# Which expert blocks of a convolution and mixture-of-experts kernel are single, double and fourfold

## The chip, the cores and the metric

The kernel runs on one core of a Trainium2 chip. The metric is the device time of one execution in microseconds (us); a time is the median of several runs. Beside it stands one execution taken with the hardware profiler, which shows every instruction of the engines: TensorE (PE, its weight loads apart as PEld), VectorE (DVE), ScalarE (ACT), GpSimd (POOL) and SyncE (SP), which issues most of the transfers.

## The reference

The input is 8 sequences of 3584 tokens with 192 channels, 28672 tokens in all, in float32. First comes a causal convolution of 7 taps with softmaxed weights, one set for each of 8 groups of 24 channels. Then each token goes through one of 8 experts of 192 x 1024 and 1024 x 192:

```python
for s in range(S):
    fresh_e = int(np.argmax(logits[b, s]))
    if s == 0 or local_gate[b, s] < 0.5:
        e = fresh_e
    else:
        e = prev_e if prev_e >= 0 else fresh_e
    prev_e = e
    ls = logits[b, s] - logits[b, s].max()
    p = np.exp(ls)
    p /= p.sum() + 1e-09
    h = np.maximum(x[b, s] @ w1[e], 0.0)
    out[b, s] = p[e] * (h @ w2[e])
```

A token either takes the best expert of its own logits or, where the local gate says so, the expert of the token before it. So the choice of expert is a running scan along the sequence.

## The kernel before

**Parts.** The tokens are worked in 16 parts of 1792 (PT). For each part the kernel convolves (`conv`, L390: 48 VectorE operations, L411, and eight on ScalarE, L401), computes logits and routes (`route`, L625; the logits with four transposes L594 on VectorE, 96 matmul records L604 on TensorE and two copies L609 on ScalarE), and scatters the rows into `slots`, a table in memory that is sorted by expert (`put`, L794: one indirect DMA on GpSimd, L801, for 128 rows, 14 for a part). The first two parts go a wider way of their own at the start (`wide`, `wide_route`).

**Units and blocks.** A unit is 128 rows of one expert in `slots`; the 28672 tokens make 229 of them here. Expert work is done in blocks: single (128 rows of one expert), pair (256) or fourfold (512). For each block the weights of the expert are loaded (`load_w`, L940, 1536 KB), the rows are loaded from `slots` (`load_rows`, L947), turned (`turn`, L383 with the copies L985), put through the hidden layer (`hidden`, L999, relu L1004) and the output layer (`output`, L1016, then L1024 on ScalarE and L1030 on VectorE, and the rows are sent out by L1034). A fourfold block comes only when all parts are routed; its hidden layer uses seven products in place of eight (`seven`, L1152; output L1196, L1206, L1209, L1214).

**Which blocks, when.** How many units are full after a part is known before the run only as a sure lower bound: of `tokens` rows over 8 experts at most 8 x (size - 1) can lie in unfilled blocks (`_sure`, L51). From it come lists for each part g: ONE[g], how many single blocks may have begun when part g is routed, up to the part EARLY - 1; TWO[g], the same for pairs, from part EARLY on and at most PAIRED; FOUR, PAIRS and REST, the fourfold, double and single blocks after the last part. Tables (`table`, L814), made on VectorE after a part, say which rows and which expert block i has. FIRST is the number of blocks before the fourfold ones. With the constants of the kernel before:

- ONE is 7, 21, 35 and then 35; 21 singles need parts 0 and 1, 14 more need part 2
- TWO is 0, 0, 0, 3, 10, 17, ... 59, 60: three pairs need part 3, then seven need each later part, and one part 12
- FIRST is 95, FOUR 13, PAIRS 4; 14 singles end it. 20 further single blocks stand in a conditional at the end and run only if rows are left.

**The order of the work.** The program is written for one fixed order on each engine. The main loop (L1359) goes block by block. Between a block's hidden layer and output, and after it, it calls `step(time)` (L1258), which issues routing and convolution work of the next parts until the costs that these generators yield (0.6 for an operation of the convolution, 0.1 to 0.8 for one of the routing) fill `time`: 4.6 for a single block, 9.6 for a pair. Routing goes first, and where it says "hop" the rest of that call is left to the convolution. `hidden` sends two scatters for a block; a pair sends a third (`put(copied)`, L1377) when over 7 are queued and a fourth (L1026) when over 12 are. At the head of each block `ensure` asks for the rows of the blocks up to three ahead:

```python
def ensure(i):
    for j in range(len(xgs) + i, min(i + AHEAD + 1, len(blocks))):
        g = blocks[j][3]
        while st["routed"] < g or any(p[0] <= g for p in to_put):
            if j > i + 2:
                return
            step(4.2)
            put()
        xgs[j] = load_rows(j)
```

`blocks[j][3]` is the part that block j needs, `to_put` the queue of scatters that aren't issued yet. A block three ahead may wait for the next call; one two ahead may not.

**Buffers that matter.** The output of a block goes to two banks (`yps_p`, two buffers); the next block's output can begin only when L1024 and L1030 have read them. The hidden layer has four banks (`hps_p`), which the logits use too.

Of the kernel before, what the change touches and what calls it, by code (L numbers as in the profile page):

```python
# [43 lines left out]
CAP = CAPU * UT  # L44
NU = (N + E * (UT - 1)) // UT
DUMMY = E * CAPU
EARLY = 3
SPARE = 2


def _sure(tokens, size):  # L51

    return max(0, -(-(tokens - E * (size - 1)) // size))
# [3 lines left out]
def _likely(tokens, size, left):  # L57
# [4 lines left out]

LAST = NPART - 1
PADS = NPART
PAIRED = 60
LEFT4 = E * (QT // 2 + UT // 8)
LEFT2 = E * (BT // 2 + UT // 8)
ONE = [_sure(min(g + 1, EARLY) * PT, UT) for g in range(NPART)]
TWO = [min(PAIRED, _sure((g + 1) * PT - ONE[-1] * UT, BT)) if g >= EARLY else 0
       for g in range(NPART)]  # L70
# [1439 lines left out]
```

## Time and profile before

| | us |
|---|---|
| median of 3 runs (1322.0 to 1323.66) | 1322.66 |
| profiled execution | 1305.35 |
| its span, first to last instruction | 1303.6 |
| VectorE busy, of the span | 846.3 |
| GpSimd busy, of the span | 523.1 |
| first hidden layer of a block (L999) | begins at 44.7 |
| first fourfold block (L1152) | begins at 910.2 |
| last logits (L604) | begin at 808.5 |
| last scatter of a part (L801) | begins at 882.2 |

The granted clock of TensorE is 0.997 of full speed over the span. The singles lie between 44.7 and 252.5 us, the pairs up to 910, the fourfold blocks up to about 1180, and the late pairs and singles after them. In the table of groups a line stands for all instructions of one source line and shape; the timeline of an engine merges equal neighbours, with the count behind the x; a bracket at its end gives the idle time in front of it and what ended it.

### The profile page before, as it was taken

What the parts mean: (1) busy time and instruction counts of PE and PEld (TensorE: products, weight loads), DVE (VectorE), ACT (ScalarE), POOL (GpSimd) and SP (SyncE); (2) the same over time, 40 slices, a digit from 0 to 9 for tenths busy, and PEclk for the clock granted to TensorE, in tenths of its full rate; (3) what the DMA queues carried; (4) which work ended last, traced back from release to release, by engine and by line L of the source; (5) the groups of instructions that cost most, each with busy time, mean ns of one, the idle gap of its engine ahead of it and who ended that gap; (6) DMA issues with size and microseconds to landing.
All of it is one profiled execution on the core that took longest, in us unless ns stands there. A gap on an engine that the chain in (4) does not pass through costs nothing.

```text
span 1303.6 us, 40830 instructions
## 1 busy us (share of the span) xinstructions
PE 1284.2 (99%) x16434; PEld 1220.6 (94%) x16434; DVE 846.3 (65%) x2526; ACT 651.1 (50%) x1482; POOL 523.1 (40%) x577
## 2 busy tenths in 40 slices
PE   9899999999999999999999999999999999999997
PEld 7799999999999999999999999999999999999997
DVE  5989898988988899998999996801333333330000
ACT  5456565544445445444454544444645556454453
POOL 3455353533435344353544534454433433322211
PEclk9999999999999999999999999999999999999999
DMA  5799999975757576575765755666323323324584
GB/s 195 285 357 415 386 384 345 398 273 202 269 203 278 196 274 244 207 280 190 281 246 204 281 193 205 214 213 235 128 87 135 122 105 140 110 94 167 212 303 164
DMA packets 63077, 300.42 MB, mean 230 GB/s; under 512 B 12064, under 2 KB 34263, under 8 KB 45474
## 3 DMA queue, kind: packets, MB, share of 16 engines
q1 hardware_dynamic: 40560, 252.54, 53.2%
q0 software_dynamic: 22320, 45.22, 9.5%
q8 instruction: 131, 2.15, 0.7%
q14 instruction: 64, 0.52, 0.1%
q10 hardware_dynamic: 2, 0.00, 0.0%
HBM read 252.12 MB, written 46.07 MB: 229 GB/s over the span
## 4 chain that ended last, share of the span: by engine, by line
PE 96%; DVE 3%; issue 0%; POOL 0%; POOLq 0%; ACT 0%; DVEq 0%
PE yps L1016 31%; PE hps L999 31%; PE ps L1196 15%; PE ps L1152 8%; PE ps L1103 4%; PE xps L383 2%; PE xps L1152 2%; PE hps L604 2%; DVE y_sb L411 1%; PE hps L233 1%; PE hps L178 0%; DVE hot L574 0%; PE hps L256 0%; PE yps L264 0%; DVE run L475 0%
## 5 line engine op out<-in xcount | busy, mean ns | idle before, releaser
L1016 PE MATMUL yps<-wb,hT 64*128 64x192 f32 x4960 | 429.8, 325 | 3.2 <-DVE o_sb L1030 2.4
L999 PE MATMUL hps<-xT,wb 64*128 64x256 f32 (+1 forms) x4560 | 425.9, 338 | 1.9 <-DVE at L503 1.2
L999 PEld LDWEIGHTS hps<-xT,wb 64*128 64x128 f32 x4560 | 378.7, 188 | 33.9 <-issue 3.9
L1016 PEld LDWEIGHTS yps<-wb,hT 64*128 64x128 f32 x4960 | 405.7, 187 | 4.6 <-DVE o_sb L1030 2.7
L411 DVE SCALAR_TENSOR_TENSOR y_sb<-x_sb,c,y_sb 128x336 f32<-128x336 f32 x672 | 375.6, 569 | 28.4 <-ACT y_sb L401 10.5
L801 POOL DMA_INDIRECT slots<-y_sb,posi x228 | 229.6, 1007 | 205.7 <-ACT xT L985 90.8
L1004 ACT ACTIVATE hT<-hps 128x512 f32<-128x512 f32 (+1 forms) x380 | 176.4, 516 | 244.5 <-PE hps L999 244.5
L1034 POOL DMA_INDIRECT out_dram<-o_sb,xg x155 | 161.5, 1042 | 276.0 <-DVE o_sb L1030 222.2
L1209 DVE SCALAR_TENSOR_TENSOR o_sb<-ps,y_sb,o_sb 128x192 f32<-128x192 f32 x74 | 28.1, 413 | 233.5 <-ACT o_sb L1206 233.5
L1214 POOL DMA_INDIRECT out_dram<-o_sb,y_sb x74 | 76.4, 1032 | 237.5 <-DVE o_sb L1209 218.7
L1196 PE MATMUL ps<-wb,x_sb 64*128 64x192 f32 x1952 | 165.0, 323 | 0.0
L1196 PEld LDWEIGHTS ps<-wb,x_sb 64*128 64x128 f32 x1952 | 159.3, 187 | 0.6
L1024 ACT ACTIVATE o_sb<-yps,xg 128x192 f32<-128x192 f32 x155 | 58.7, 418 | 178.4 <-PE yps L1016 178.3
L985 ACT COPY xT<-xps 128x256 f32<-128x256 f32 (+3 forms) x380 | 142.0, 374 | 10.6 <-PE xps L383 4.8
L1030 DVE SCALAR_TENSOR_TENSOR o_sb<-yps,xg,o_sb 128x192 f32<-128x192 f32 x155 | 58.6, 410 | 77.2 <-ACT o_sb L1024 77.0
L1206 ACT ACTIVATE o_sb<-ps,y_sb 128x192 f32<-128x192 f32 x74 | 27.9, 418 | 102.2 <-PE ps L1196 97.7
L1152 PE MATMUL ps<-x_sb,wb 64*128 64x256 f32 x624 | 73.7, 376 | 0.0
L1152 PEld LDWEIGHTS ps<-x_sb,wb 64*128 64x128 f32 x624 | 59.0, 187 | 7.3
L401 ACT ACTIVATE y_sb<-x_sb,c 128x336 f32<-128x336 f32 x112 | 61.9, 578 | 0.0
L1103 PE MATMUL ps<-x_sb,wb 64*128 64x128 f32 (+1 forms) x864 | 61.6, 295 | 0.0
L1103 PEld LDWEIGHTS ps<-x_sb,wb 64*128 64x128 f32 x864 | 59.4, 188 | 0.9 <-issue 0.2
L1083 ACT COPY x_sb<-xps 128x128 f32<-128x128 f32 (+5 forms) x124 | 58.7, 473 | 2.3
(277 smaller groups left out, 1043.5 us busy)
## 6 DMA issues: line engine op xcount, KB each, us to landing
wb<-in_w_dram SPq DMA_DIRECT2D x122, 1536.0 KB
x_sb<-in_x_dram SPq DMA_DIRECT2D x14, 1920.0 KB
xg<-slots SPq DMA_DIRECT2D x60, 195.0 KB
wb<-in_w_dram SPq DMA_DIRECT2D x12, 512.0 KB
y_sb<-slots SPq DMA_DIRECT2D x13, 390.0 KB
slots<-y_sb,posi POOLq DMA_INDIRECT x228
xg<-slots SPq DMA_DIRECT2D x33, 97.5 KB
x_sb<-in_xb_dram SPq DMA_DIRECT2D x4, 768.0 KB
```

The lines of the kernel that those rows point to most:

```text
L401: nc.scalar.activation(cols(h), chans(h, 0), Act.Copy, scale=c[:, h, 0:1])
L411: nc.vector.scalar_tensor_tensor(cols(h), chans(h, k), c[:, h, k:k + 1], cols(h), Alu.mult, Alu.add)
L801: ins = nc.gpsimd.indirect_dma_start(out=slots[:, :], in_=rows, in_offset=None, out_offset=bass.IndirectOffsetOnAxis(ap=to, axis=0)).ins
L985: copied = nc.scalar.copy(a, b)
L999: nc.tensor.matmul(hps[half][:, j, w], lhsT=wb[rows, f0:f0 + P], rhs=xT[rows, d, w], start=(d == 0 and j == 0), stop=(d == KD - 1), skip_g ...
L1004: relu = nc.scalar.activation(hT[:, m:m + 2, w], hps[half][:, :, w], Act.Relu)
L1016: nc.tensor.matmul(yps[half][:, k * D:(k + 1) * D], lhsT=hT[rows, m, k * P:(k + 1) * P], rhs=wb[rows, WA + m * D:WA + (m + 1) * D], start= ...
L1034: sent = nc.gpsimd.indirect_dma_start(out=out, in_=o_sb[:, k, :], in_offset=None, out_offset=bass.IndirectOffsetOnAxis(ap=xg.bitcast(I32)[ ...
L1103: nc.tensor.matmul(hps[:, half, j, :], lhsT=wb[rows, f0:f0 + P], rhs=xT[rows, d, :], start=(d == 0 and j == 0), stop=(d == KD - 1), skip_g ...
L1152: ins = nc.tensor.matmul(to[:, half, j, :], lhsT=b[rows, j * P:(j + 1) * P], rhs=a[rows, :], start=(first and j == 0), stop=True, skip_gro ...
L1196: ins = nc.tensor.matmul(yps[:, half, k * D:(k + 1) * D], lhsT=h[two][rows, side, j, k * P:(k + 1) * P], rhs=wb[rows, WA + f * D:WA + (f + ...
L1214: sent = nc.gpsimd.indirect_dma_start(out=out, in_=o_sb[:, k, :], in_offset=None, out_offset=bass.IndirectOffsetOnAxis(ap=xg.bitcast(I32)[ ...
```

## The change

Two constants change. The rest follows from them by the formulas of the code.

```diff
-EARLY = 3
+EARLY = 2
 SPARE = 2
...
-PAIRED = 60
+PAIRED = 63
```

The formulas between them and the blocks stay:

```python
ONE = [_sure(min(g + 1, EARLY) * PT, UT) for g in range(NPART)]
TWO = [min(PAIRED, _sure((g + 1) * PT - ONE[-1] * UT, BT)) if g >= EARLY else 0
       for g in range(NPART)]
PAST = ONE[-1] * UT + TWO[-1] * BT
FOUR = _likely(N - PAST, QT, LEFT4)
```

ONE becomes 7, 21 and then 21. TWO becomes 0, 0, 3, 10, 17, ... 59, 63: three pairs need part 2, seven part 3, and so on. FIRST becomes 84, FOUR 15; PAIRS stays 4 and the singles at the end stay 14. The rows that the blocks before FIRST take go from 19840 to 18816.

## The prediction

> **What bounds the kernel now.** I read the page first: busy time, the 40 slices and the chain. TensorE is busy from end to end, and the chain of work that ended last is TensorE's own.
>
> ```profile
> PE 1284.2 (99%) x16434; PEld 1220.6 (94%) x16434; DVE 846.3 (65%) x2526; ACT 651.1 (50%) x1482; POOL 523.1 (40%) x577
> PE 96%; DVE 3%; issue 0%; POOL 0%; POOLq 0%; ACT 0%; DVEq 0%
> ```
>
> A busy TensorE can hide waits, so next the waits of TensorE alone, from the start to the end. They sum to about 10 us and all but 1.5 us of them lie in the first 65 us. There is nothing left here to take away; there is much that could be added.
>
> ```profile
> PE yps L1016 <- DVE o_sb L1030: 2.4, 1, 2.4
> PE xps L383 <- DMA xg<-slots: 1.3, 1, 1.3
> ```
>
> Third, the windows by stage (stretch, then busy us of PE, PEld, DVE, ACT, POOL, then clock, DMA share and GB/s). VectorE, which does the convolution and the routing, has 275 of 300 us filled in the middle of the run. It is the one engine that can't take a burst of work without somebody waiting.
>
> ```profile
> 80.00:171.40 91.40, 90.74 (x1535) 89.75 (x1534) 80.59 (x275) 51.31 (x162) 41.57 (x43) 1.00 0.97 378
> 500.00:800.00 300.00, 300.00 (x3766) 282.56 (x3764) 274.61 (x817) 147.38 (x335) 137.55 (x132) 1.00 0.67 240
> 910.00:1180.00 270.00, 270.00 (x3058) 254.65 (x3056) 90.82 (x155) 146.62 (x199) 95.52 (x106) 1.00 0.33 116
> ```
>
> Last, TensorE's timeline, for what one block costs (start, us, engine, line). The first matmuls of a block's hidden layer come 5.445 us apart for singles (149.66 to 193.22 is eight blocks), 10.66 for pairs and 20.42 for blocks of 512.
>
> ```profile
> 149.66 2.83 PE L999 MATMUL hps<-xT,wb 64*128 64x128 f32 x46
> 155.10 2.83 PE L999 MATMUL hps<-xT,wb 64*128 64x128 f32 x46
> ...
> 604.38 5.34 PE L999 MATMUL hps<-xT,wb 64*128 64x256 f32 x48
> 615.04 5.35 PE L999 MATMUL hps<-xT,wb 64*128 64x256 f32 x48
> ...
> 910.24 2.75 PE L1152 MATMUL ps<-x_sb,wb 64*128 64x256 f32 x24
> 930.66 2.75 PE L1152 MATMUL ps<-x_sb,wb 64*128 64x256 f32 x24
> ```
>
> **What the Trainium skill says.** PSUM — Partial Sum Buffer, section Engine vs sequencer instructions: the queues of VectorE, ScalarE and GpSimd are strictly first in, first out, and matmuls start in program order. The trace agrees: nine convolution operations that stood ahead of one output's L1030 on VectorE (58.91 to 64.10) are what the 2.41 us wait below was for. TensorE: Matmul & The Clock Gate, section What's actually happening: after an idle window of about 3.4 us the array falls to half rate until a busy window of that length. The trace agrees: behind that one wait the granted clock was 0.68 on average from 64.6 to 68 us, and 29 matmuls took 4.00 us where 30 take 2.65.
>
> ```profile
> 64.57 4.00 PE L1016 MATMUL yps<-wb,hT 64*128 64x192 f32 x29 [2.41 <-DVE o_sb L1030]
> ```
>
> **The change, part by part.** *The blocks.* With the constants worked out, singles go from 35 to 21, pairs from 60 to 63, blocks of 512 from 13 to 15; the 4 late pairs and 14 late singles stay, and so do the 229 units in all. By the periods above: -14 x 5.445 + 3 x 10.66 + 2 x 20.42 = -76.2 + 32.0 + 40.8 = **-3.4 us** of TensorE. Nine loads of 1536 KB of weights go as well. TensorE hardly waits for them today (1.5 us of unnamed waits after 80 us), so they are worth between -1.5 and 0; I take 0. One table (L814) is still made for each part up to the cap, so VectorE's own sum is unchanged but for the time at which it is asked for.
>
> *Whose rows a pair needs.* Before, the 14 singles 21 to 34 use part 2, and part 3 is first needed by block 35. After, three pairs (21 to 23) use part 2, and block 24 already needs part 3. That is 8 units of 5.4 us earlier. From the later parts on (unit 41, 55, ...) the needs are as before. So the question is what the planner has issued by then. I follow step() with the costs that its generators yield. Up to block 20 nothing differs. Route 3 puts its 14 scatters in the queue in block 18; blocks 19 and 20 send two each, as the trace shows two L801 per single from 164.26 on:
>
> ```profile
> 169.70 1.04 POOL L801 DMA_INDIRECT slots<-y_sb,posi  x1 [1.23 <-ACT xT L985]
> 171.05 0.96 POOL L801 DMA_INDIRECT slots<-y_sb,posi  x1 [0.31 <-issue]
> ```
>
> Ten are left. Block 21, now a pair, sends three. Seven are left when ensure(22) asks for block 24. At i=21 the test j > i + 2 let it off; at i=22 it doesn't. The loop has to run seven times step(4.2) and put(), one behind the other, with no matmul of a block between them. Before, singles 21 to 25 send the ten, and the loop never runs anywhere. This is the step that decides.
>
> *What the seven rounds hold.* Convolution 4 has 48 operations: 20 are issued by block 20 and 16 in block 21. Rounds 1 and 2 issue its last 12. Round 3 begins route 4: four transposes (L594), then 3 operations of convolution 5. Round 4 puts the logits' matmuls (L604) into TensorE's queue and the copies L609 into ScalarE's, then 7 operations. Round 5 is 4.3 us of routing. Round 6 is 0.4 and 7 operations. Round 7 puts the exponential L662 into ScalarE's queue and 4.2 us of routing on VectorE. All of it stands ahead of block 22.
>
> *Its price.* Durations from VectorE's timeline: nine L411 in 5.15 to 5.28 us, so 0.577 each; the four L594 1.84 + 1.43.
>
> ```profile
> 172.25 0.41 DVE L1030 SCALAR_TENSOR_TENSOR o_sb<-yps,xg,o_sb 128x192 f32<-128x192 f32 x1
> 172.57 5.15 DVE L411 SCALAR_TENSOR_TENSOR y_sb<-x_sb,c,y_sb 128x336 f32<-128x336 f32 x9
> ...
> 191.30 1.84 DVE L594 STREAM_TRANSPOSE z<-y_sb 128x768 f32<-128x768 f32 x2
> ...
> 194.10 1.43 DVE L594 STREAM_TRANSPOSE z<-y_sb 128x768 f32<-128x768 f32 x2
> ```
>
> Block 21 begins at 171.5 on TensorE, as in the trace, and ends at 182.2. Its two L1030 end at about 183.7. From there VectorE has, in order: 6 operations 3.5 (to 187.1), rounds 1 and 2, 6.9 (194.0), transposes 3.3 (197.3), 10 operations 5.8 (203.1), routing of round 5, 5.0 by the same rows of route 3 at 145.0 (208.1), round 6 4.4 (212.5), round 7 4.6 (217.1), block 22's own steps of 4.8 and 1.2, 6.3 (223.4), and block 22's L1030, 0.7: 224.1.
> First wait: L604 stands next in TensorE's queue and needs the transposes: 182.3 to 197.3, **15.0 us**. Second: its 1.6 us, the hidden layer and the transposes of block 22 are through by 204.5 at full clock and 206.5 at half clock; the relu behind L662 comes at 208.4, because L662 waits for L637 in round 5 (207.5). So 2 to 4 us. Third: block 23's output needs the bank that block 22's L1030 reads at 224.1, and TensorE is there at about 219.4: some 5 us. In sum: without waits TensorE would begin block 23's output at 182.2 + 10.66 + 5.4 + 1.6 = 199.9; it begins at 224.2. **24.3 us**. The half clock after the third wait isn't absorbed by a later one: 1.4 by the row at 64.57 to 3.4 by the skill's window; I take 1.7. Block 23 leaves VectorE 10.0 us of work per 10.66, its L1030 is out at 234.5 and block 24's output comes at 236.9: no fourth wait.
> The seven scatters cost 7 x 1.27 on GpSimd (from 186.4), and block 24's rows, waiting behind them on SP, are needed only at 229: nothing. The weights of block 25 behind them have 40 us: nothing.
>
> *The work done early* buys nothing back: no wait of TensorE is left later that it could shorten.
>
> *The end of the pairs.* FIRST goes from block 95 to 84 and lies 8 units earlier. By the same count the last table comes in block 78, six pairs ahead (seven before), and at ensure(82) one scatter of part 15 is left: one forced put, 1.3 us on GpSimd, with 16 us until its rows are turned. Nothing; if that cover were gone, 1 to 4.
>
> **Sum.** -3.4 + 24.3 + 1.7 = +22.6 us. The profiled execution took 1305.35 (span 1303.6 and 1.75 around it): 1328.0. The median of the runs, 1322.66, stands 17.3 above it; the trace doesn't show why, and I carry that over unchanged: **1345.3**.
>
> **Rivals.** Only the first wait: if VectorE gets through rounds 4 to 7 while TensorE catches up, it is -3.4 + 15.0 + 1.7, 1336. For it: the second and third are ends of long sums. Against: VectorE's queue is strict, and the sum has no idle piece in it. More than forecast: part 5's input late, each wait followed by a full slow window, a fourth wait at block 24, where there are only 2.4 us to spare: some 8 us more, 1353. On the other side: no wait at all, 1322.66 - 3.4 = 1319.3. Its mechanism is one: the queue of scatters is empty when block 24 is asked for, so that no round is forced. Its place is ensure(22), its price the whole 26 us, and it decides from seven more scatters sent by block 21. Against it stands the trace's two per single. That the change doesn't do what it says I exclude: the input's experts, counted, fill all 15 blocks of 512, 4 pairs and 14 singles, so the conditional blocks at the end stay empty as before.
>
> **Numbers.** Forecast 0.71, first wait only 0.13, more 0.10, none 0.04, and 0.02 for something between none and one. A measurement tells no more than 0.2% (2.6 us) from no change. Faster 0.04, same 0.02, slower 0.94. The range reaches to the smaller case and to the larger one's middle: 1335 to 1353.
>
> **What would show it.** TensorE's waits: 15 us in front of L604, released by L594; about 5 in front of L1016, released by L1030; 2 to 4 in front of L1016 behind ScalarE, all between 180 and 226 us, with a granted clock below 1 there. Seven L801 in a row near 187. Then no wait until the end, and 84 early blocks. I am wrong if L604 at about 182 waits less than 10 us, or if TensorE waits again after block 24.

## The result, and the profile after

The changed kernel takes **1341.11 us** (median of 4 runs, 1339.65 to 1343.4) beside 1323.16 for the kernel before (4 runs, 1322.0 to 1328.92): a ratio of 1.0128, with a 95% interval of 1.0099 to 1.0156. (All ratios here are taken over the single runs; the quotient of two medians can differ by up to 0.0015.) It is slower by 18 us, where +22.6 had been summed. The profiled execution took 1340.49 us, its span is 1338.8.

The page of the changed kernel, first the busy times, then the chain of work that ended last:

```profile
PE 1294.6 (97%) x16082; PEld 1254.2 (94%) x16082; DVE 856.8 (64%) x2523; ACT 650.7 (49%) x1416; POOL 529.1 (40%) x585
PE 83%; issue 8%; DVE 5%; POOL 2%; DMA 1%; ACT 0%; another core or an unknown queue 0%; POOLq 0%; SPq 0%; DVEq 0%; ACTq 0%
```

TensorE has 352 matmul records fewer than before and is still the engine that ends last. VectorE's share of the chain went from 3% to 5%: the path now leaves TensorE for a stretch. The 8% under "issue" say nothing of the loss: they lie behind 1176 us, in the late blocks, where the chain is followed another way, and TensorE is busy there for 152.7 of 154 us. TensorE's waits in the changed kernel (us in total, times, longest) say who it waits for:

```profile
PE hps L604 <- DVE z L594: 13.1, 2, 12.9
PE yps L1016 <- DVE o_sb L1030: 6.9, 2, 4.7
PE yps L1016 <- issue: 2.5, 7, 0.5
PE yps L1016 <- ACT hT L1004: 2.4, 1, 2.4
```

Three of the four are the three waits of the prediction, in kind and roughly in size (of the two waits for L1030 the one of 4.7 us; the other, 2.2, lies at 66 us, where the kernel before has one too). The third line is something else: seven short pauses for which the profile has no releaser. They return below. Where the three lie, TensorE's timeline of the changed kernel shows (start, us, engine, line, shapes, count, and in the bracket the idle time before and what ended it):

```profile
181.85 5.42 PE L1016 MATMUL yps<-wb,hT 64*128 64x192 f32 x63
200.19 1.40 PE L604 MATMUL hps<-z,wg 64*32 64x128 f32 x8 [12.91 <-DVE z L594]
201.81 3.23 PE L604 MATMUL hps<-z,wg 64*32 64x128 f32 x88 [0.23 <-DVE z L594]
...
213.15 5.47 PE L1016 MATMUL yps<-wb,hT 64*128 64x192 f32 x64 [2.36 <-ACT hT L1004]
218.45 5.35 PE L999 MATMUL hps<-xT,wb 64*128 64x256 f32 x48
...
229.12 6.98 PE L1016 MATMUL yps<-wb,hT 64*128 64x192 f32 x61 [4.71 <-DVE o_sb L1030]
```

Block 21's output ends at 187.27 and block 23's begins at 229.12: 41.85 us. Without waits these are one pair, one hidden layer and the logits, 17.7 us by the prediction's durations, so 24.15 us are lost up to there. VectorE's timeline over the same stretch shows what it had to do first:

```profile
188.25 10.78 DVE L411 SCALAR_TENSOR_TENSOR y_sb<-x_sb,c,y_sb 128x336 f32<-128x336 f32 x18
199.06 3.16 DVE L594 STREAM_TRANSPOSE z<-y_sb 128x768 f32<-128x768 f32 x4
202.14 5.86 DVE L411 SCALAR_TENSOR_TENSOR y_sb<-x_sb,c,y_sb 128x336 f32<-128x336 f32 x10
...
213.27 4.07 DVE L411 SCALAR_TENSOR_TENSOR y_sb<-x_sb,c,y_sb 128x336 f32<-128x336 f32 x7
...
228.32 0.74 DVE L1030 SCALAR_TENSOR_TENSOR o_sb<-yps,xg,o_sb 128x192 f32<-128x192 f32 x2
```

The 18 convolution operations are the 6 of block 21 and the 12 of rounds 1 and 2; then come the four transposes, the 3 + 7 operations of rounds 3 and 4, and the 7 of round 6. The order counted from the planner's costs is the order on the chip. The second wait comes by way of ScalarE, whose relu of block 22 (L1004) stands behind the routing's exponential L662, which waits for VectorE:

```profile
212.31 0.30 ACT L662 ACTIVATE ex<-ex 128x112 f32<-128x112 f32 x1 [5.86 <-DVE eq L637]
212.52 2.04 ACT L1004 ACTIVATE hT<-hps 128x512 f32<-128x512 f32 x4
```

On GpSimd the seven forced scatters stand in one row, from 191.20 to 200.11; the first and the last of them:

```profile
191.20 0.97 POOL L801 DMA_INDIRECT slots<-y_sb,posi  x1 [0.30 <-issue]
...
199.15 0.96 POOL L801 DMA_INDIRECT slots<-y_sb,posi  x1 [0.30 <-issue]
```

Last, the windows of the changed kernel over the two slow stretches (stretch, length, busy us of PE, PEld, DVE, ACT, POOL, granted clock, DMA share, GB/s):

```profile
191.60:205.30 13.70, 4.76 (x98) 3.20 (x100) 13.14 (x23) 1.27 (x4) 6.67 (x7) 0.50 0.31 93
229.20:232.60 3.40, 3.40 (x22) 3.40 (x24) 3.12 (x15) 0.00 (x0) 2.79 (x3) 0.50 0.31 111
```

TensorE has half its clock through the second part of the first wait and for all the logits behind it, and for 3.4 us behind the third wait: 22 matmuls where full speed would have given some forty.

### The profile page after: what moved, and what is told of

Its sections match the earlier page's. It is cut to its first block, busy times and chain, and to the rows that moved or that the text cites. A ratio compares the mean times of both kernels' runs of the same rounds, so it can differ in the third digit from the quotient of the medians.

```text
span 1338.8 us, 39944 instructions
## 1 busy us (share of the span) xinstructions
PE 1294.6 (97%) x16082; PEld 1254.2 (94%) x16082; DVE 856.8 (64%) x2523; ACT 650.7 (49%) x1416; POOL 529.1 (40%) x585
## 4 chain that ended last, share of the span: by engine, by line
PE 83%; issue 8%; DVE 5%; POOL 2%; DMA 1%; ACT 0%; another core or an unknown queue 0%; POOLq 0%; SPq 0%; DVEq 0%; ACTq 0%
PE yps L1016 29%; PE hps L999 28%; PE ps L1196 11%; PE ps L1152 8%; DVE y_sb L411 2%; PE xps L383 2%; PE xps L1152 2%; PE hps L604 2%; POOL out_dram L1214 1%; PE ps L1103 1%; DMA out_dram<-o_sb,y_sb 1%; DMA wb<-in_w_dram 1%; PE hps L233 1%; PE hps L178 0%; DVE hot L574 0%
## 5 line engine op out<-in xcount | busy, mean ns | idle before, releaser
L1016 PE MATMUL yps<-wb,hT 64*128 64x192 f32 x4704 | 417.8, 326 | 12.5 <-DVE o_sb L1030 6.9
L999 PE MATMUL hps<-xT,wb 64*128 64x256 f32 (+1 forms) x4032 | 409.1, 351 | 2.1 <-DVE at L503 1.2
L1016 PEld LDWEIGHTS yps<-wb,hT 64*128 64x128 f32 x4704 | 391.9, 188 | 18.2 <-issue 7.8
L411 DVE SCALAR_TENSOR_TENSOR y_sb<-x_sb,c,y_sb 128x336 f32<-128x336 f32 x672 | 376.7, 570 | 31.4 <-ACT y_sb L401 12.9
L999 PEld LDWEIGHTS hps<-xT,wb 64*128 64x128 f32 x4032 | 373.7, 187 | 22.0 <-issue 4.4
L1004 ACT ACTIVATE hT<-hps 128x512 f32<-128x512 f32 (+1 forms) x336 | 166.0, 541 | 261.6 <-PE hps L999 155.1
L1196 PE MATMUL ps<-wb,x_sb 64*128 64x192 f32 x2144 | 183.4, 323 | 0.0
L1196 PEld LDWEIGHTS ps<-wb,x_sb 64*128 64x128 f32 x2144 | 177.6, 187 | 0.2 <-issue 0.2
L985 ACT COPY xT<-xps 128x256 f32<-128x256 f32 (+3 forms) x336 | 130.9, 390 | 14.5 <-remote 5.3
L1030 DVE SCALAR_TENSOR_TENSOR o_sb<-yps,xg,o_sb 128x192 f32<-128x192 f32 x147 | 55.0, 409 | 67.1 <-ACT o_sb L1024 65.4
L1152 PE MATMUL ps<-x_sb,wb 64*128 64x256 f32 x720 | 92.2, 376 | 0.0
L1152 PEld LDWEIGHTS ps<-x_sb,wb 64*128 64x128 f32 x720 | 82.9, 187 | 0.0
L1083 ACT COPY x_sb<-xps 64x512 f32<-64x512 f32 (+6 forms) x132 | 64.2, 487 | 2.5
L1103 PEld LDWEIGHTS ps<-x_sb,wb 64*128 64x128 f32 x864 | 59.9, 188 | 1.3 <-ACT o_sb L1206 1.2
```

Source lines behind the costliest of these rows:

```text
L411: nc.vector.scalar_tensor_tensor(cols(h), chans(h, k), c[:, h, k:k + 1], cols(h), Alu.mult, Alu.add)
L985: copied = nc.scalar.copy(a, b)
L999: nc.tensor.matmul(hps[half][:, j, w], lhsT=wb[rows, f0:f0 + P], rhs=xT[rows, d, w], start=(d == 0 and j == 0), stop=(d == KD - 1), skip_g ...
L1004: relu = nc.scalar.activation(hT[:, m:m + 2, w], hps[half][:, :, w], Act.Relu)
L1016: nc.tensor.matmul(yps[half][:, k * D:(k + 1) * D], lhsT=hT[rows, m, k * P:(k + 1) * P], rhs=wb[rows, WA + m * D:WA + (m + 1) * D], start= ...
L1083: copied = nc.scalar.copy(a, b)
```

## The experiments

Two theories stood after the result. *Forced steps*: the loop in `ensure(22)` puts seven steps on VectorE ahead of block 22, and this is the whole price. *Scatters*: what costs is the row of scatters on GpSimd, or the lack of a fuller queue, and the steps are incidental. A second question had been open since the prediction: why the profiled execution of before took 1305.35 us when its timed runs took 1322.66.

The experiments ran on four chips in turn, each time with the kernel before beside them: 1323.72 us on the first chip (27 runs), 1305.35, 1305.18 and 1305.42 on the second to fourth (25, 17 and 25 runs). Differences in us are to these medians. On which chip the runs of the result and the first profile were taken is not on record.

### First chip, where the kernel before takes 1323.72

**The kernel before once more**, unchanged.

> The kernel before, unchanged, profiled once more. The changed kernel's profile fits the forecast wait by wait, yet its span is 35.1 us above the one execution of before that was profiled (1303.6), while the timed medians lie 18 us apart. Theory: that execution was an unusually smooth one, and a usual one has some 12 to 17 us of holes in TensorE's work with no releaser ('issue'), spread over the run; then this profile has a span near 1320, with no wait at L604. Rival: profiles of before are always near 1304 and the timed runs have something outside the span; then 1304 again. Ratio to before 1.000 in both.

1323.09 us, 0.9998 [0.9986, 1.001], span 1322.8. Here is an execution of before as the timed runs have it, 19.2 us longer than the one profiled first. TensorE's waits in it:

```profile
PE hps L604 <- issue: 3.0, 10, 0.4
PE yps L1016 <- ACT hT L1004: 2.9, 1, 2.9
...
PE yps L1016 <- issue: 2.3, 6, 0.5
```

No wait explains 19 us. The mean of a matmul is the same as in the first profile (L999 of 256 rows 377 ns in both, L1016 326 and 325), but the stream has small pauses without a releaser, spread through the stage with scatters: the first fourfold block begins at 929.16 instead of 910.24, and behind it only another 0.3 us are lost. Those that the list of waits names come to about 6 us, against 1.5 in the first profile; the rest is finer and shows only as matmuls that stand farther apart (TensorE's busy time, in which overlapping matmuls count once, is 1298.6 us instead of 1284.2 for the same 16434 matmuls). So the 17.3 us that the prediction could not see lie inside the span, in TensorE's own stream, and not around it. In what follows "pauses" means both kinds.

**The changed kernel, with the loop issuing scatters but no steps** unless a routing is really due:

```diff
-                step(4.2)
+                if st["routed"] < g:
+                    step(4.2)
                 put()
```

> The changed kernel, but the loop of ensure calls step only where the part isn't routed yet; where only scatters are left it calls put alone. So the seven scatters at block 22 go out in a row as before, without the 29 us of VectorE work. Theory (the forced steps are the price, 26 us; the scatters cost nothing): no wait at L604, none at L1016 behind L1030 between 180 and 230 us; 26 us below the changed kernel, so about 1315 timed, 0.994 of before (3.4 us of fewer blocks, the rest fewer holes). Rival A (the early need of part 3 itself, the scatters and the late rows, is the price): TensorE waits for the rows of block 24 and the time stays above 1330. Rival B (pairs so early cost for another reason): 1323 to 1330 with a new wait.

1342.19 us, 1.0128 [1.0105, 1.0151]: as slow as the changed kernel. It had been expected at about 1315. The wait at L604 is gone from the trace, and still nothing is gained; pauses took its place:

```profile
PE yps L1016 <- issue: 13.6, 24, 1.6
```

They lie in blocks beside rows of scatters: block 29 takes 17.02 us and the last pair 26.57 where a pair takes 10.67. The clock is at half around them, for 30.7 us in three stretches, which adds to the loss.

**The kernel before with 15 blocks of 512** (35 singles, 56 pairs; the late pairs and singles as before): the second half of the change alone.

```diff
-PAIRED = 60
+PAIRED = 56
```

> The kernel before with PAIRED 56 in place of 60: 35 singles, 56 pairs, 15 fourfold blocks. It has the early end of the pairs (147 units) without the early need of part 3. By the counts no round is forced at the start; at the end 11 scatters of part 15 go in one row at the second block before the fourfold ones (1 in the changed kernel, none before). Blocks: -4 x 10.66 + 2 x 20.42 = -1.8 us. Theory: the row of scatters takes 11 x 1.27 = 14 us from 3.6 us into the block, landing and loading the rows some 5 more, and TensorE needs them 15.7 us into it, so it waits some 7 us before it turns the first fourfold block's rows: +5 us against before, 1.004. Rival (the end of the pairs is covered): -2 us, 0.998.

1338.43 us, 1.0096 [1.0071, 1.0121]: +14.7 where +5 was expected. Its last pair takes 26.53 us, beside a row of 13 scatters (871.21 to 887.3). TensorE's timeline there:

```profile
879.42 0.47 PE L1016 MATMUL yps<-wb,hT 64*128 64x192 f32 x1 [1.08 <-issue]
880.84 0.47 PE L1016 MATMUL yps<-wb,hT 64*128 64x192 f32 x1 [0.94 <-issue]
882.22 0.48 PE L1016 MATMUL yps<-wb,hT 64*128 64x192 f32 x1 [0.91 <-issue]
```

Single matmuls a good microsecond apart, and nothing that they are seen to wait for. Taken by itself this looks as if the row of scatters starved TensorE.

**The changed kernel with short steps in the loop**:

```diff
-                step(4.2)
+                step(1.2)
                 put()
```

> The changed kernel with step(1.2) in place of step(4.2) in the loop of ensure: still seven rounds, but only the last 12 operations of convolution 4 are forced (6.9 us on VectorE), and no logits come into TensorE's queue between the blocks 21 and 22. Theory (the price is the VectorE work that stands ahead of block 22's output): no wait at L604; one wait of 1 to 4 us at L1016 behind L1030; timed 22 to 25 us below the changed kernel, 1316 to 1319. Rival (the seven rounds as such, their scatters and the places where they fall, cost): above 1330.

1336.04 us, 1.0081 [1.0055, 1.0106]. Expected were 1316 to 1319. There is no wait at L604, but block 22, with the logits' 2.8 us in it, takes 19.31 us with pauses of 0.3 to 0.95 us at 195 to 201, and the last pair 21.56. On this chip the wait and the pauses can't be told apart by the time alone, so each suspect is put by itself below.

### Second chip, where the kernel before takes 1305.35

**The steps alone**, in the kernel before: seven of them at block 22, without scatters, where nothing needs them.

```diff
         st["block"] = i
+        if i == 22:
+            for _ in range(7):
+                step(4.2)
         ensure(i)
```

> The kernel before (35 singles, 60 pairs) with seven step(4.2) at the head of block 22 and no scatter with them. Nothing is needed early, no row of scatters. Theory (VectorE work ahead of block 22 is a price of its own): L604 waits some 17 us for L594, block 23's output some 9 us for L1030, a half clock behind it: +26 to 28 us against before, 1350, 1.020. Rival (the price of the changed kernel is the row of scatters, the forced steps ran beside it): under +10 us.

1334.52 us, 1.0226 [1.021, 1.0242], so +29.2. TensorE's waits:

```profile
PE hps L604 <- DVE z L594: 15.1, 2, 14.9
PE yps L1016 <- DVE o_sb L1030: 9.8, 2, 7.5
```

The steps alone bring the first and the third wait. They cost 3 us more than the 26 of the forecast's two terms; the third wait is 7.5 us instead of 4.7, and block 22 is a single here, with half a pair's matmuls to work on while VectorE is behind, which may be why.

**A row alone**, in the kernel before: ten scatters at one point, without steps, where no block waits for their rows yet.

```diff
         st["block"] = i
+        if i == 37:
+            for _ in range(10):
+                put()
         ensure(i)
```

> The kernel before with ten of its own scatters sent in one row at the head of block 37, in place of three or four each in the blocks 37 to 40. No block needs their rows for a long time, no VectorE work is moved. In the runs before, blocks with a row of scatters were longer than usual: 13 in a row 15.9 us, 7 in a row 8.4 us over two blocks, 5 in a row 6.4 us. Theory A (a row of scatters on GpSimd by itself slows TensorE, by some 1.2 us for each): TensorE has holes without a releaser in block 37 or 38, 12 us in all, 1335, 1.009. Theory B (what cost there was the wait for the rows): no change, 1.000.

1304.93 us, 0.9992 [0.9982, 1.0002]: no effect. Twelve scatters stand in a row from 278.78 to 294.71 (first GpSimd's timeline, two of them), and TensorE goes through blocks 37 and 38 in 10.67 and 10.66 us (then TensorE's):

```profile
280.05 1.31 POOL L801 DMA_INDIRECT slots<-y_sb,posi  x1 [0.30 <-issue]
...
290.99 0.96 POOL L801 DMA_INDIRECT slots<-y_sb,posi  x1 [0.30 <-issue]
```

```profile
278.93 5.42 PE L1016 MATMUL yps<-wb,hT 64*128 64x192 f32 x64
284.19 5.34 PE L999 MATMUL hps<-xT,wb 64*128 64x256 f32 x48
289.60 5.42 PE L1016 MATMUL yps<-wb,hT 64*128 64x192 f32 x64
```

So a row by itself does not starve TensorE here. What the first chip showed is bound to that chip, or to its condition then.

**67 pairs and 13 blocks of 512**, the changed kernel with other pairs:

```diff
-PAIRED = 63
+PAIRED = 67
```

> The changed kernel with PAIRED 67 in place of 63: 21 singles, 67 pairs, 13 fourfold blocks, so the end of the pairs lies at unit 155 as before, and only the early need of part 3 is left. Theory (nearly all of the price is at block 22): blocks -14 x 5.445 + 7 x 10.66 = -1.6 us against before in place of -3.4, all waits of the changed kernel between 187 and 229 us stay, so 1.8 us above the changed kernel: 1343, 1.014 of before. Rival (the earlier end of the pairs holds a good part of the price): 1330 to 1338.

1328.18 us, 1.0171 [1.0156, 1.0187], +22.8. The three waits are there as before (12.9, 2.0, 4.7). With the end of the pairs where it was before, the early need of part 3 alone has all of the loss. (The 15 blocks of 512 alone, +14.7 on the first chip, were not tried on a chip without pauses.)

**Scatters spaced otherwise**, in the kernel before: of a pair's two in the hidden layer, both after the second half of it.

```diff
-            hT = hidden(n, wbs[i], xT, (1, 1) if i else (0, 0))
+            hT = hidden(n, wbs[i], xT, (0, 2) if i else (0, 0))
```

> The kernel before, but a pair's two scatters both go behind its second relu, not one behind each: so two sends of the last block and the next scatters don't stand in one row on GpSimd. Theory A of the row: some of the 12 to 19 us of holes in a usual execution go, 3 to 8 us: 1316 to 1320, 0.996. Rival (those holes have another cause): 1323, 1.000, or slower where the second relu's scatters now form a row with the third.

1305.43 us, 0.9997 [0.9988, 1.0007]. Where a scatter stands inside a block doesn't matter here. The pauses that this was to shorten are not there on this chip, so it says nothing about them.

### Third chip, where the kernel before takes 1305.18

**The changed kernel once more**, unchanged.

> The changed kernel once more, beside the kernel before on whatever chip this is; before took 1323 us on one chip and 1305 on another, the latter with no holes without a releaser. Theory: the waits at block 22 and 23 and the half clock behind them cost about 23 to 26 us on either, less 3.4 us for the blocks. Where before takes 1305, the changed kernel takes 1327 (1.017); where it takes 1323, 1341 (1.013) as at first, since both lose time to holes there. Rival (the changed kernel's time doesn't depend on the chip): 1341 in both.

1327.26 us, 1.0177 [1.0159, 1.0194]: **+22.1 us**, beside the forecast's sum of +22.6. TensorE's waits:

```profile
PE hps L604 <- DVE z L594: 13.1, 2, 12.9
PE yps L1016 <- DVE o_sb L1030: 7.1, 2, 4.7
PE yps L1016 <- ACT hT L1004: 2.1, 1, 2.1
```

The same three waits, and no pauses of L1016 without a releaser.

**Scatters without steps once more** (the edit of the first chip's second run).

> The changed kernel with put alone in ensure where only scatters are left (e2 again). Theory: without the holes that a row of scatters brings on one chip, nothing is left of the price, and the fewer blocks show: where before takes 1305, this takes 1302 (0.997) with no wait of TensorE over 2.5 us after 80 us; where before takes 1323, 1342 (1.013) as in e2. Rival (VectorE's work comes too late at the end of the pairs in any case): 1310 or more where before takes 1305, with a wait in front of the first fourfold block.

1314.56 us, 1.008 [1.0066, 1.0094], so +9.4, where 1302 had been expected: leaving out the steps gains 12.7 us against the run above, not the whole 26. No wait at L604 is left; but TensorE's waits have new ones at their head, and its timeline shows where the longest lies:

```profile
PE xps L383 <- DMA y_sb<-slots: 8.3, 1, 8.3
PE xps L383 <- DMA xg<-slots: 2.9, 2, 1.5
```

```profile
854.53 5.35 PE L999 MATMUL hps<-xT,wb 64*128 64x256 f32 x48
...
868.23 1.12 PE L383 MATMUL xps<-ident,y_sb 64*128 64x64 f32 x16 [8.35 <-DMA y_sb<-slots]
869.11 7.23 PE L1016 MATMUL yps<-wb,hT 64*128 64x192 f32 x64
```

This is the end of the pairs, where the rows of the first fourfold block are turned. The load of these rows starts on SP only behind the last row of scatters, which begins at 848.92 on GpSimd:

```profile
864.34 1.20 SPq L947 DMA_DIRECT2D y_sb<-slots  x2
```

The clock is at half for 10.2 us around this wait (the 64 matmuls of L1016 take 7.23 us instead of 5.42). Of the second line, one wait of 1.4 us lies at 198.89, in front of block 24's rows, so the row of scatters at block 22 is not free where its rows are due. With 2.3 us for the half clock (1.8 in these 64 matmuls, 0.5 in the 16 in front of them) the sum is -3.4 + 8.3 + 1.4 + 2.3 = 8.6 of the 9.4. The steps forced at block 22 are, in the changed kernel, also work done in advance: without them VectorE reaches the last routing later, and the last part's scatters come out too late for the fourfold blocks: the positions of the last part's rows (L769) are made at 827.49 here and at 819.40 in the run above, though the pairs end some 24 us earlier here.

The same program had its long blocks on the first chip beside rows of scatters. Here the same rows are in the trace (five at 264.22 to 270.23, and thirteen from 848.92), and TensorE goes on at full pace beside them: block 29 takes 10.77 us, and the 48 matmuls above, from 854.53 on, take 5.35. So neither the rows nor their place make the pauses by themselves.

**The row alone once more**: 1304.65 us, 0.9999 [0.999, 1.0008]; again no effect.

> The kernel before with ten of its own scatters in one row at block 37 (f3 again), which changed nothing where before takes 1305. Theory: a row of scatters stops TensorE's supply on the chip where before takes 1323 and not on the other: 1335 (1.009) with holes without a releaser in block 37 or 38 there, 1305 (1.000) here. Rival (the long blocks of e2 and e3 came from the late rows, not from the row of scatters): 1.000 on both.

### Fourth chip, where the kernel before takes 1305.42

**A version that has neither wait**: the loop without steps, one scatter more in each of blocks 19 and 20, so that fewer are left for block 21 and 22, and 65 pairs with 14 blocks of 512, so that the fourfold blocks begin two pairs later.

```diff
-PAIRED = 63
+PAIRED = 65
...
-            for _ in range(shares[two] if n == KT else (0, sum(shares))[two]):
+            for _ in range(shares[two] if n == KT else (0, sum(shares) + (st["block"] in (19, 20)))[two]):
...
-                step(4.2)
+                if st["routed"] < g:
+                    step(4.2)
                 put()
```

> The changed kernel with put alone in ensure where only scatters are left, PAIRED 65 (14 fourfold blocks, pairs end at unit 151) and three scatters in place of two in the blocks 19 and 20. By the counts the row at block 22 has six scatters in place of seven and the one before the fourfold blocks four in place of eleven. In g2 the rows of block 24 were 1.4 us late and those of the first fourfold block 8.4 us; with 1.27 us for each scatter less they come 0.2 us late and in time. Blocks: -14 x 5.445 + 5 x 10.66 + 20.42 = -2.5 us. Theory (nothing else was left of the price): where before takes 1305, 1303 (0.998), no wait of TensorE over 1 us after 80 us. Rival (VectorE or the rows are late elsewhere): 1306 or more. Where before takes 1323, the rows of scatters make it slower, 1330 to 1340.

**1302.2 us**, 0.9977 [0.997, 0.9984]: 3.2 us faster than the kernel before. The changed kernel was not run on this chip; on the third it took 1327.26. Its longest waits of TensorE, and the one matmul group behind the longest of them in the timeline:

```profile
PE yps L1016 <- DVE o_sb L1030: 2.2, 1, 2.2
PE xps L383 <- DMA xg<-slots: 1.7, 2, 1.5
```

```profile
63.29 2.70 PE L1016 MATMUL yps<-wb,hT 64*128 64x192 f32 x29 [2.21 <-DVE o_sb L1030]
```

No wait above 1 us lies after 80 us. By the periods the blocks bring -76.2 + 5 x 10.66 + 20.42 = -2.5 us. And the 29 matmuls behind the early wait take 2.70 us here, not 4.00 as in the first profile of before: the clock stays at full, which is worth another 1.3 us in that execution. So the 3.2 us are not proof of the 2.5 alone. This version was not tried on the first chip.

## Why the prediction was right, and where it was off

It said slower, by a forced round of steps at block 22, and 1345.3; measured were 1341.1.

- *The step that decides.* Right: seven scatters left, seven rounds. The rival without a forced round is out. That the steps and not the scatters make the waits is shown by adding each alone: seven steps cost 29.2 us, ten scatters nothing at a place where no rows are due. Scatters whose rows are due did cost 1.4 us at block 24 once the steps were gone.
- *The first wait*, 15.0 forecast, 12.9 measured. The sum behind it ran from the end of block 21's output to the transposes; VectorE's 18 + 4 operations came out as counted (10.78 and 3.16 us), only TensorE was let go after the first part of the transposes: L604 starts at 200.19, L594 ends at 202.2. What the wait lacked came back behind it: the logits ran at half clock, which the forecast had as a range only (logits and hidden layer by 204.5 or 206.5).
- *The second and third wait*, 2 to 4 and about 5: 2.4 and 4.7. The strict order of VectorE's and ScalarE's queues, which the Trainium skill states (PSUM — Partial Sum Buffer, Engine vs sequencer instructions), is what carried these two ends of long sums. The trace agrees: block 22's L1030 starts at 228.32, behind all of the routing, though ScalarE's half of that output was done at 219.4. The rival with the first wait only is out.
- *All three together*, 24.3: 24.15 by the timeline of the changed kernel, 24.1 on the third chip.
- *The half clock behind the third wait*, 1.7: the 61 matmuls take 6.98 us, and at the pace of a full output (64 in 5.42) they take 5.17, so 1.8; on the third chip 7.27 us, so 2.1. Half clock is also in the logits behind the first wait, 4.9 us instead of 1.6, but the later waits swallow that.
- *The blocks*, -3.4: taken alone nowhere. The kernels with 63 and with 67 pairs (-3.4 and -1.6 by the periods) measured +22.1 and +22.8, on two chips, with the same waits; this agrees in sign, and the difference is within the spread of the runs.
- *No fourth wait, nothing at the end of the pairs*: right for the changed kernel. But the reason given, cover of 16 us, holds only with the forced steps in place. "If that cover were gone, 1 to 4" was too small, and "the work done early buys nothing back" was wrong: where the steps were taken out, a wait of 8.35 us came up there, with the half clock around it.

**The term that was mis-sized** is the last of the sum: "the trace doesn't show why, and I carry that over unchanged". The 17.3 us are pauses of TensorE that the kernel before has on one chip and not on three others; the first profile is like those of the three, the timed runs beside it like those of the one. With the medians of the third chip, without pauses, the sum runs 1305.18 + 22.1, and the changed kernel's pauses are 1341.11 - 1327.26 = 13.9 us, not 17.3. Of the 4.2 us of error 3.5 are this term, 0.5 the sum and 0.2 the starting value. That this term was off by no more than 3.5 us is luck: nothing in the prediction says why the change should leave it alone, and it did not.

Where the changed kernel has fewer pauses can be read from the starts of its blocks. From block 21 to the first pair the kernel before takes 81.2 us in the first profile (171.33 to 252.53) and 85.1 in the first chip's (177.53 to 262.59), so 3.9 us of pauses; from its own block 21 to a pair at much the same time, with the three waits in between, the changed kernel takes 83.0 us both on the third chip (170.07 to 253.07) and in the first profile of it (176.06 to 259.04), so none. Why there are none, the idle time or the pairs in place of singles, is not shown.

What is open: what the pauses are. On that chip they lie beside rows of scatters (blocks of 17, 19 and 26 us there), and two rows put in on purpose on other chips had no effect, nor had the rows of the very same program; a row put in by itself was not tried on that chip. Whether it is the chip or its condition in those minutes is open too, and so is whether the last version is faster there.

## What to carry to other kernels

Where the order of the work is written out by a planner, look for the loop that catches up when a deadline is missed, and count what it has left to issue at the new deadline: it runs on one engine's queue in one piece, and every later end on this engine moves with it. Let a catch-up loop issue only what the deadline needs (here the scatters), and follow work that it no longer does early to the next deadline, here 670 us later, before its removal is called free: doing only this left +9.4 us here. When timed runs stand above the profiled execution by about as much as the effect in question, here 17.3 beside 22.6 us, profile again until an execution with the longer time is at hand, since a carried-over difference is a term of the sum like any other.

## What the runs showed of the hardware

- The same program, unchanged, took 1323 us on one chip and 1305 on three others. The difference for one program was 18.0 us (before), 13.9 (changed) and 27.6 (scatters without steps, 1342.19 and 1314.56): it depends on the program, so that a ratio measured on one chip (1.0128) is not the ratio on another (1.0177). Whether the chip or its condition at the time makes the difference can't be told here.
- Half clock came after less than the idle window of about 3.4 us that the Trainium skill gives (TensorE: Matmul & The Clock Gate, What's actually happening), so the prediction's row at 64.57 agrees with the page in the half rate but not in the length of the wait. The length of a wait doesn't decide either: half clock followed waits of 2.18 us (15 blocks of 512) and 2.41 (the first profile of before), and did not follow waits of 2.21 (the last version) and 2.36 (the second wait of the changed kernel). In each trace the changes of the granted clock lie whole multiples of 3.41 us apart, and what tells the cases apart is how long TensorE was busy in the one such stretch just before. In before it was busy for 1.24 of 3.41 us, and the next stretch has half the clock; in the last version 1.72 was the least, and the clock stayed (stretch, length, then as above):

```profile
62.40:65.81 3.41, 1.24 (x14) 1.24 (x16) 3.27 (x8) 1.49 (x5) 1.02 (x1) 1.00 0.99 406
65.81:69.22 3.41, 3.41 (x28) 3.41 (x27) 3.23 (x7) 0.89 (x2) 1.93 (x3) 0.50 1.02 415
```

```profile
59.36:62.77 3.41, 1.72 (x29) 1.42 (x26) 3.23 (x7) 2.73 (x9) 0.00 (x0) 1.00 1.11 431
```

For the two other waits the figures are 1.23 us (half clock) and 2.09 (none). This is read from single waits; among the pauses of the first chip half clock came with more busy time than that.
- The way back agrees with the page, which asks for a busy window of that length: from the end of a wait to full clock the changed kernel took 3.5 us behind its third wait, the kernel before 4.65 us behind its one of 2.41. A wait can so cost more than its own length: 1.3 us more behind 2.41, 1.8 and 2.1 more behind 4.7.
